# Output products and value products of two groups interleaved by tiling on TensorE

## The chip, the cores and the metric

The kernel runs on one core of a Trainium2 chip. The metric is the time of one execution on the device in microseconds (us), as the median of several runs. Five engines work side by side, each through its own queue in order: TensorE (PE, with its weight loads as PEld), VectorE (DVE), ScalarE (ACT), GpSimd (POOL) and SyncE (SP). PE writes into PSUM, from where ACT and DVE read; POOL and SP issue the transfers here.

## The reference

`x` is 8 x 4224 x 192, `weight_gen` 8 x 4224 x 8 x 7. A dynamic convolution (a softmax over 7 taps for each of 8 heads, applied to the last 7 rows of `x`) is followed by a gated product:

```python
w = np.exp(weight_gen - weight_gen.max(-1, keepdims=True)); w = w / (w.sum(-1, keepdims=True) + 1e-09)
x = np.einsum('bshk,bskhg->bshg', w, x_unf).reshape(B, S, D)   # x_unf: the last 7 rows
gate_pre = sum(conv_w[k] * xp[:, k:k + S, :] for k in range(5))  # xp: x with 4 zero rows ahead
gate = 1.0 / (1.0 + np.exp(-gate_pre))
val = x @ w_val
return gate * val @ w_out
```

## The kernel before

The sequence is cut into 36 **groups** of 118 rows, all 8 batches together. A group `m` goes through these steps:

- `load_x` (POOL, L410; three buffers `xt`) and `load_t` (SP, L424; two buffers `tb`) bring the rows of `x` and a banded matrix of softmax weights. The softmax itself runs ahead in ten parts on DVE and ACT; `spread` (ACT, L320) lays its result out in `zt`, a store (L327; SP for the first three parts, POOL after) puts it into the DRAM tensor `zd`, and `load_t` reads it from there.
- `bank` (PE, L437): the dynamic convolution as four sets of 32 small matmuls in a tiling of four column tiles, each set into a PSUM tile `pa` of which there are three. `evac` (ACT, L448 to L455) copies them to `A`, `B` and `S`; `move` (POOL, L464 and L466) transfers slices of `S` into `A` and `B`.
- `tap0` (ACT, L478), four `tap` (DVE, L483) and `sigm` (ACT, L488) make the gate, in `aA` for channels 0 to 127 and in `aB` for the other 64 (two batch halves above each other).
- `val` (PE): the product with `w_val` into the PSUM tiles `v2` and `v01` of which there is one each. L497 uses two column tiles of 64, L499 and L501 the whole array, L504 two row tiles of 64.
- `gv` (DVE, L511 and L513): gate times value, in place in `aA` and `aB`.
- `omm(k)`, `k` = 0 and 1 (PE): the product with `w_out`, two batches of each half at a time, into the PSUM tile `po`, of which there is one. Its part with `aA` (L524, four matmuls) uses the whole array, its part with `aB` (L531, four matmuls) two row tiles of 64. `oev(k)` (ACT, L546) copies `po` to `ot`, and `store` (SP, L555) writes the result.

Matrix products in float32 take two passes: the profile shows two instructions for each matmul.

The order on every engine is fixed by a planner, the class `Order`: steps are added with an engine, a duration, a key and the steps they depend on, and `run` plays them through with its own figures. On the engine that is free first it takes, among the steps that could begin within `SLACK` of the earliest, the one with the smallest key. `SWITCH` is what it adds when PE changes its tiling (`mode`), `RATE` and `LAND` are its figures for transfers. The order that comes out is what the engines execute; the waits are real semaphores. `val` depends on the `gv` of the group before, since `v2` and `v01` have one buffer; `omm(0)` depends on `gv` of its own group and on the last `oev` of the group before; `omm(1)` on `oev(0)`.

At the start POOL and DVE share the conversion of the two weight matrices (L210 to L221), which arrive as 64-bit numbers.

Of the kernel before, what the change touches and what calls it, by code (L numbers as in the profile page):

```python
# [16 lines left out]
class Order:  # L17
# [4 lines left out]
    SWITCH = 0.1  # L22
    SEM = 0.08
    RATE = 260e3
    LAND = {"SP": 2.8, "ACT": 2.8, "POOL": 3.8}
# [16 lines left out]
    def run(self):  # L42
# [6 lines left out]
        free, mode, dma = {}, {}, 0.0  # L49
# [6 lines left out]
        while done < len(self.ops):  # L56
            best = None
            for eng, c in open_.items():
                if not c:
                    continue  # L60
                t = free.get(eng, 0.0)
                first = min(max(t, o.ready) for _, o in c)
                n, o = min(((n, o) for n, o in c if max(t, o.ready) <= first + self.SLACK), key=lambda x: (x[1].key, x[0]))
                s = max(t, o.ready)
                if best is None or s < best[0]:
                    best = (s, n, o)
# [9 lines left out]
            if o.bytes:  # L76
                dma = max(dma, e + 0.8) + o.bytes / self.RATE
                o.end = dma + self.LAND[o.eng]
# [11 lines left out]
def tile_dynconv_gated_moe(  # L90
# [9 lines left out]
    nc = tc.nc  # L100
# [279 lines left out]
    class Group:  # L380
# [109 lines left out]
        def val(self):  # L490
            n = HB * self.n
            v2 = self.v2 = ps_v.tile([P, 512], FP32, name="v2")
            v01 = self.v01 = ps_v.tile([P, 2, 512], FP32, name="v01")
            A, Bt = self.part(0, HALO), self.part(1, HALO)
            A = [A[:, HB * u:HB * u + HB] for u in range(2)]
            for u in range(2):
                nc.tensor.matmul(out=v2[HD * u:HD * u + HD, 0:n], lhsT=wvm, rhs=A[u], start=True, stop=False,  # L497
                                 tile_position=(0, HD * u))
            nc.tensor.matmul(out=v2[:, 0:n], lhsT=wvd, rhs=Bt, start=False, stop=True)  # L499
            for u in range(2):  # L500
                nc.tensor.matmul(out=v01[:, u, 0:n], lhsT=wva, rhs=A[u], start=True, stop=False)  # L501
            for u in range(2):
                hs = slice(HD * u, HD * u + HD)
                nc.tensor.matmul(out=v01[:, u, 0:n], lhsT=wvb[hs], rhs=Bt[hs], start=False, stop=True,  # L504
# [10 lines left out]
        def omm(self, k):  # L515

            n = self.n
            po = self.po = ps_o.tile([P, 2, 512], FP32, name="po")

            def a_part(first):  # L520
                for u in range(2):
                    for t in range(2):
                        c = n * (HB * u + 2 * k + t)
                        nc.tensor.matmul(out=po[0:n, u, D * t:D * t + D], lhsT=self.aA[:, c:c + n], rhs=woa,  # L524
                                         start=first and t == 0, stop=not first, skip_group_check=True)

            def b_part(first):
                for t in range(2):
                    for u in range(2):
                        hs, c = slice(HD * u, HD * u + HD), n * (2 * k + t)  # L530
                        nc.tensor.matmul(out=po[0:n, u, D * t:D * t + D], lhsT=self.aB[hs, c:c + n], rhs=wob[hs],  # L531
                                         start=first and t == 0, stop=not first, skip_group_check=True,
                                         tile_position=(HD * u, 0))

            if k == 0:
                b_part(True)
                a_part(False)
            else:
                a_part(True)
                b_part(False)  # L540
# [84 lines left out]

    for i in range(3):
        soft_part(i)
    late_clear.behind.append(soft[1]["exp"])
    for m, gp in enumerate(gr):
# [58 lines left out]
        val = add("PE", 5 * mm(HB * n), m + 1.5, gp.val, [*full[0], *full[1], *placed, *dep(m - 1, "gv")], mode=("64c", "64r"))  # L688
# [39 lines left out]
```

## Time and profile before

| | us |
|---|---|
| median of 3 runs (lowest, highest) | 588.81 (587.95, 588.96) |
| profiled execution, its own time | 587.95 |
| its span | 586.2 |
| PE busy | 484.9 (83%) |
| DVE busy | 438.5 (75%) |
| ACT busy | 345.0 (59%) |
| POOL busy | 330.2 (56%) |
| L437 PE MATMUL `pa` x4608 | 140.5 |
| L524 PE MATMUL `po` x576 | 117.2 |
| L531 PE MATMUL `po` x576 | 68.6 |
| L497, L499, L501, L504 PE MATMUL `v` | 38.0, 39.3, 63.6, 38.1 |
| L546 ACT COPY `ot` x72, mean of one | 57.8, 0.803 |

Busy time counts what an engine executes, not what it waits; the ends of matmuls are modelled, so a row of a block can end 0.07 us after the next block has begun. A timeline row has start, length, engine, line, operation and count, and in brackets how long the engine stood idle ahead of it and what ended that.

### The profile page before, as it was taken

How to read it: one execution, taken by the hardware profiler on the slowest of the kernel's cores; microseconds unless marked ns; L12 is line 12 of the kernel's file. 1: busy time of each engine (PE TensorE's matmuls, PEld its weight loads, DVE VectorE, ACT ScalarE, POOL GpSimd, SP SyncE). 2: the span in 40 equal slices, each digit the busy share in tenths (PEclk: the TensorE clock that was granted, in tenths of full speed). 3: DMA queues.
4: the chain of work that ended last, by engine and by line, in shares of the span. 5: the costliest groups of instructions: out<-in, count | busy, mean ns of one | idle time of the engine just before them, and what ended most of it. 6: DMA issues, size and time to landing. Idle time of an engine off the chain costs nothing.

```text
span 586.2 us, 15839 instructions
## 1 busy us (share of the span) xinstructions
PE 484.9 (83%) x6278; PEld 327.0 (56%) x6278; DVE 438.5 (75%) x488; ACT 345.0 (59%) x533; POOL 330.2 (56%) x613
## 2 busy tenths in 40 slices
PE   2033868599848988999979997998999999999994
PEld 1033535386525764566746673765766675767653
DVE  6776396679857299898887889878975679667780
ACT  4435554478535667458666766586585656546641
POOL 9535956256470666657457455677576687522410
PEclk7557879799987999999979998999999999999999
DMA  5989689738799998879997989799789868775222
GB/s 156 213 239 242 144 223 257 200 99 236 216 236 228 283 266 243 207 207 246 290 259 187 267 217 275 212 261 252 194 217 259 248 158 200 205 183 164 66 60 89
DMA packets 105869, 123.17 MB, mean 210 GB/s; under 512 B 17938, under 2 KB 95615, under 8 KB 103107
## 3 DMA queue, kind: packets, MB, share of 16 engines
q1 hardware_dynamic: 79779, 65.40, 42.5%
q0 software_dynamic: 26016, 56.75, 36.1%
q8 instruction: 50, 0.82, 0.6%
q14 instruction: 24, 0.20, 0.1%
HBM read 64.55 MB, written 51.43 MB: 198 GB/s over the span
## 4 chain that ended last, share of the span: by engine, by line
PE 40%; DMA 30%; POOL 13%; issue 8%; ACT 4%; DVE 2%; SPq 1%; POOLq 0%; ACTq 0%; DVEq 0%
DMA zd<-zt 13%; PE po L524 10%; PE pa L437 10%; POOL xt L410 7%; DMA A<-S 6%; PE po L531 5%; DMA xt<-in_x_dram 5%; PE v L501 5%; DMA tb<-zd 3%; PE v L499 3%; PE v L504 3%; PE v L497 3%; POOL A L464 2%; DMA raw_c<-cd 1%; POOL B L466 1%
## 5 line engine op out<-in xcount | busy, mean ns | idle before, releaser
L483 DVE SCALAR_TENSOR_TENSOR aA<-A,wf,aA 128x944 f32<-128x944 f32 (+1 forms) x144 | 171.6, 1192 | 26.6 <-ACT aA L478 22.8
L437 PE MATMUL pa<-tb,xt 128*32 128x122 f32 (+1 forms) x4608 | 140.5, 276 | 48.8 <-DMA tb<-zd 43.1
L410 POOL DMA_DIRECT2D xt<-in_x_dram x272 | 143.8, 549 | 44.0 <-DMA A<-S 8.7
L437 PEld LDWEIGHTS pa<-tb,xt 128*32 128x32 f32 x4608 | 127.7, 110 | 64.0 <-issue 56.1
L483 DVE SCALAR_TENSOR_TENSOR aB<-B,wf,aB 128x472 f32<-128x472 f32 (+1 forms) x144 | 101.2, 703 | 46.2 <-ACT aB L478 39.0
L466 POOL DMA_DIRECT2D B<-S x144 | 74.7, 525 | 95.8 <-ACT B L451 83.5
L524 PE MATMUL po<-wf,aA 128*118 128x192 f32 (+1 forms) x576 | 117.2, 349 | 11.8 <-DVE aA L511 9.4
L524 PEld LDWEIGHTS po<-wf,aA 128*118 128x118 f32 (+1 forms) x576 | 94.6, 188 | 43.2 <-issue 20.1
L464 POOL DMA_DIRECT2D A<-S x144 | 74.2, 521 | 69.2 <-DMA zd<-zt 36.9
L546 ACT COPY ot<-po 118x768 f32<-118x768 f32 (+1 forms) x72 | 57.8, 803 | 82.3 <-PE po L531 49.4
L531 PE MATMUL po<-wf,aB 64*118 64x192 f32 (+1 forms) x576 | 68.6, 358 | 26.6 <-ACT ot L546 16.8
L531 PEld LDWEIGHTS po<-wf,aB 64*118 64x118 f32 (+1 forms) x576 | 45.8, 183 | 42.6 <-ACT ot L546 18.9
L501 PE MATMUL v<-A,wva 128*128 128x472 f32 (+1 forms) x144 | 63.6, 562 | 0.0
L455 ACT COPY S<-pa 64x488 f32<-64x488 f32 (+1 forms) x72 | 40.5, 562 | 31.1 <-PE pa L437 30.6
L488 ACT ACTIVATE aA<-aA 128x944 f32<-128x944 f32 (+1 forms) x36 | 35.5, 986 | 32.5 <-DVE aA L483 32.5
L511 DVE TENSOR_TENSOR aA<-v,aA 128x944 f32<-128x944 f32 (+1 forms) x36 | 40.7, 1130 | 13.7 <-PE v L504 8.1
L320 ACT COPY zt<-wt 128x192 f32<-128x192 f32 (+3 forms) x100 | 39.1, 461 | 17.5 <-DVE wt L308 11.4
L478 ACT ACTIVATE aA<-A,wf 128x944 f32<-128x944 f32 (+1 forms) x36 | 38.9, 1081 | 14.2 <-DMA A<-S 14.2
L501 PEld LDWEIGHTS v<-A,wva 128*128 128x128 f32 x144 | 27.7, 192 | 31.0 <-issue 30.4
L448 ACT COPY A<-pa 128x488 f32<-128x488 f32 (+1 forms) x72 | 40.5, 565 | 6.5 <-PE pa L437 5.3
L497 PE MATMUL v<-A,wvm 128*64 128x472 f32 (+1 forms) x144 | 38.0, 605 | 7.1 <-DMA A<-S 5.2
L499 PE MATMUL v<-B,wvd 128*128 128x472 f32 (+1 forms) x72 | 39.3, 627 | 0.0
(60 smaller groups left out, 367.5 us busy)
## 6 DMA issues: line engine op xcount, KB each, us to landing
xt<-in_x_dram POOLq DMA_DIRECT2D x272, 96.0 KB, 4.2
tb<-zd SPq DMA_DIRECT2D x285, 88.0 KB
out_dram<-ot SPq DMA_DIRECT2D x35, 672.0 KB
zd<-zt POOLq DMA_DIRECT2D x14, 1104.0 KB, 8.1
wt<-in_weight_gen_dram SPq DMA_DIRECT2D x6, 1120.0 KB
zd<-zt POOLq DMA_DIRECT2D x6, 920.0 KB, 7.5
A<-S POOLq DMA_DIRECT2D x140, 30.5 KB, 4.4
B<-S POOLq DMA_DIRECT2D x140, 15.2 KB, 4.8
```

Of the source, the lines that this page charges most:

```text
L410: nc.gpsimd.dma_start(out=self.xb[:, j, 0:D], in_=src)
L437: nc.tensor.matmul(out=pa[Q * c:Q * c + Q, w * j:w * j + w], lhsT=self.xb[:, u * HB + j, C * h:C * h + Q], rhs=self.t[:, u * HB + j, PAD / ...
L464: nc.gpsimd.dma_start(out=self.A[q:q + n], in_=self.S[p:p + n])
L466: nc.gpsimd.dma_start(out=self.B[HD * u + q:HD * u + q + n], in_=self.S[p:p + n, w * u:w * u + w])
L483: nc.vector.scalar_tensor_tensor(out=a, in0=self.part(g, j), scalar=cw[:, g, j:j + 1], in1=a, op0=ALU.mult, op1=ALU.add)
L497: nc.tensor.matmul(out=v2[HD * u:HD * u + HD, 0:n], lhsT=wvm, rhs=A[u], start=True, stop=False, tile_position=(0, HD * u))
L499: nc.tensor.matmul(out=v2[:, 0:n], lhsT=wvd, rhs=Bt, start=False, stop=True)
L501: nc.tensor.matmul(out=v01[:, u, 0:n], lhsT=wva, rhs=A[u], start=True, stop=False)
L511: nc.vector.tensor_tensor(out=a, in0=self.v01[:, :, 0:n], in1=a, op=ALU.mult)
L524: nc.tensor.matmul(out=po[0:n, u, D * t:D * t + D], lhsT=self.aA[:, c:c + n], rhs=woa, start=first and t == 0, stop=not first, skip_group_ ...
L531: nc.tensor.matmul(out=po[0:n, u, D * t:D * t + D], lhsT=self.aB[hs, c:c + n], rhs=wob[hs], start=first and t == 0, stop=not first, skip_g ...
L546: nc.scalar.copy(out=self.ot[0:n, :, 2 * k:2 * k + 2, :].rearrange("p u t d -> p u (t d)"), in_=self.po[0:n, :, 0:2 * D])
```

## The change

`val` is split into `val_c` (column tiles), `val_a` (whole array) and `val_b` (row tiles), and `omm` into `out_a` (whole array) and `out_b` (row tiles). A function `output(m, last)` adds the output products of a group; the two calls for group `m - 1` stand inside the value product of group `m`: after `val_a` comes `out_a(0)`, `out_b(0)`, then `val_b`, then `out_b(1)`, `out_a(1)`. `gv` of `aB` depends on `val_a` alone, that of `aA` on `val_b`. The planner counts a change of tiling already when it chooses, with 0.19 us in place of 0.1; it keeps a transfer figure for each queue, where it had one for all, and its rate and landing times are lower.

```diff
-    SWITCH = 0.1
+    SWITCH = 0.19
...
-    RATE = 260e3
-    LAND = {"SP": 2.8, "ACT": 2.8, "POOL": 3.8}
+    RATE = 200e3
+    LAND = {"SP": 2.4, "ACT": 2.4, "POOL": 3.2}
...
-                first = min(max(t, o.ready) for _, o in c)
-                n, o = min(((n, o) for n, o in c if max(t, o.ready) <= first + self.SLACK), key=lambda x: (x[1].key, x[0]))
-                s = max(t, o.ready)
+                now = mode.get(eng)
+                at = [(max(t, o.ready), (o.mode is not None and o.mode[0] != now) * self.SWITCH, n, o) for n, o in c]
+                first = min(s + w for s, w, _, _ in at)
+                s, _, n, o = min((a for a in at if a[0] + a[1] <= first + self.SLACK), key=lambda x: (x[3].key, x[2]))
...
-                dma = max(dma, e + 0.8) + o.bytes / self.RATE
-                o.end = dma + self.LAND[o.eng]
+                dma[o.eng] = max(dma.get(o.eng, 0.0), e + 0.8) + o.bytes / self.RATE
+                o.end = dma[o.eng] + self.LAND[o.eng]
...
+    def output(m, last):
...
+        d, gp = T[m], gr[m]
+        n, k = gp.n, len(d.setdefault("oev", []))
+        free = dep(m - 1, "oev")[-1:] if k == 0 else d["oev"][-1:]
+        a, f = m + 2.52 + 0.03 * k, (gp.out_a, gp.out_b)
+        o = [last] if last else []
+        for i, c in enumerate((k, 1 - k)):
+            o.append(add("PE", (4, 2)[c] * mm(D), a + 0.01 * i, lambda c=c, i=i: f[c](k, i == 0),
+                         [d["gv"][1 - c], conv["o"], *(free if i == 0 else [])], mode=(("128",), ("64r",))[c], behind=o[-1:]))
+        lent = dep(m - 3, "store") if m != 2 else [conv["o"], conv["v"]]
+        d["oev"].append(add("ACT", act(4 * D, True), m + 1.2, lambda: gp.oev(k), [o[-1], *(lent if k == 0 else [])]))
...
-        val = add("PE", 5 * mm(HB * n), m + 1.5, gp.val, [*full[0], *full[1], *placed, *dep(m - 1, "gv")], mode=("64c", "64r"))
-        gv = [add("DVE", dve(size[g]), m + 2.0, lambda gp=gp, g=g: gp.gv(g), [val, sg[g]]) for g in (1, 0)]
...
-        for k in range(2):
-            o.append(add("PE", 6 * mm(D), m + 2.1 + 0.3 * k, lambda gp=gp, k=k: gp.omm(k),
-                         [*gv, conv["o"], *(evs[-1:] if k else dep(m - 1, "oev")[-1:])], mode=(("64r", "128"), ("128", "64r"))[k]))
...
+        gv1 = dep(m - 1, "gv")
+        vc = add("PE", mm(HB * n), m + 1.5, gp.val_c, [*full[0], *full[1], *placed, *gv1], mode=("64c",))
+        va = add("PE", 3 * mm(HB * n), m + 1.51, gp.val_a, [*gv1], mode=("128",), behind=[vc])
+        mid = output(m - 1, va) if m else va
+        vb = add("PE", mm(HB * n), m + 1.54, gp.val_b, [], mode=("64r",), behind=[mid])
+        if m:
+            output(m - 1, vb)
+        d["gv"] = [add("DVE", dve(size[g]), m + 2.0, lambda gp=gp, g=g: gp.gv(g), [(vb, va)[g], sg[g]]) for g in (1, 0)]
+        d["useA"], d["useB"] = [va, tp[0][-1]], [vb, tp[1][-1]]
+    output(NM - 1, output(NM - 1, None))
```

Since the planner's figures and its choice change, the order changes on all engines, not at the moved products alone. Two places follow. In the rows of an order `x4` counts equal instructions in a row, and each matmul stands once.

PE, around the value product 22 (counted from 0), before: L437 is a bank, L531 and L524 are the `aB` and `aA` parts of an output product, L497 to L504 the value product.

```order
L437 MATMUL pa<-tb_76,xt_82 32x122 x64
L531 MATMUL po<-wf,aB 118x192 x4
L524 MATMUL po<-wf,aA 118x192 x4
L497 MATMUL v_3912<-A,wvm 64x472 x2
L499 MATMUL v_3912<-B,wvd 128x472
L501 MATMUL v_3913<-A,wva 128x472 x2
L504 MATMUL v_3913<-B,wvb 128x472 x2
L524 MATMUL po<-wf,aA 118x192 x4
L531 MATMUL po<-wf,aB 118x192 x4
```

The same engine with the change, around the same value product (the second L498): L438 is the bank, L498, L503 and L506, L512 are `val_c`, `val_a`, `val_b`, L531 is `out_a` and L542 `out_b`.

```order
L438 MATMUL pa<-tb_75,xt_81 32x122 x64
L438 MATMUL pa<-tb_76,xt_82 32x122 x64
L498 MATMUL v_3801<-A,wvm 64x472 x2
L503 MATMUL v_3801<-B,wvd 128x472
L506 MATMUL v_3810<-A,wva 128x472 x2
L531 MATMUL po<-wf,aA 118x192 x4
L542 MATMUL po<-wf,aB 118x192 x4
L512 MATMUL v_3810<-B,wvb 128x472 x2
L542 MATMUL po<-wf,aB 118x192 x4
L531 MATMUL po<-wf,aA 118x192 x4
L498 MATMUL v_3876<-A,wvm 64x472 x2
```

Blocks of one tiling now stand beside each other (L503, L506 and L531; L542, L512 and L542), two banks follow each other, and the two output products of a group are `val_b` apart where a whole value product or a bank lay between them.

POOL at the start of the program, before: `xt` are loads of `x`, `B<-S` and `A<-S` are moves (the first eight are the first group's), L214 to L220 convert `w_out`.

```order
L466 DMA B<-S 8x488 x2
L410 DMA xt_82<-in_x_dram 128x1x192 x8
L466 DMA B<-S 8x488 x2
L464 DMA A<-S 8x976 x4
L410 DMA xt_80<-in_x_dram 128x1x192 x8
L214 TENSOR_SCALAR wf<-wf 128x2x192
L466 DMA B<-S 8x488 x4
L218 TENSOR_SCALAR aA<-aA 128x2x192
L219 TENSOR_SCALAR aA<-aA 128x2x192
L220 TENSOR_TENSOR wf<-wf,aA 128x2x192
```

The same place with the change; the conversion has the lines L215 to L221, the loads L411, the moves L467 and L465.

```order
L411 DMA xt_81<-in_x_dram 128x1x192 x8
L215 TENSOR_SCALAR wf<-wf 128x2x192
L411 DMA xt_82<-in_x_dram 128x1x192 x8
L219 TENSOR_SCALAR aA<-aA 128x2x192
L220 TENSOR_SCALAR aA<-aA 128x2x192
L221 TENSOR_TENSOR wf<-wf,aA 128x2x192
L467 DMA B<-S 8x488 x4
L411 DMA xt_80<-in_x_dram 128x1x192 x2
L465 DMA A<-S 8x976 x4
```

The conversion of `w_out` has moved ahead of the first group's moves, and these stand behind one more set of loads.

More of the change, by code (lines that the diff above doesn't have):

```diff
@@ L48, in run @@
                 d.users.append((o, False))
-        free, mode, dma = {}, {}, 0.0
+        free, mode, dma = {}, {}, {}
         open_ = {}
@@ L488, in sigm, with rows_of, val_c, val_a @@
             nc.scalar.activation(out=a, in_=a, func=AF.Sigmoid)
-        def val(self):
+        def rows_of(self, u):
+            return self.part(0, HALO)[:, HB * u:HB * u + HB]
+        def val_c(self):
+            self.v2 = ps_v.tile([P, 512], FP32, name="v2")
+            for u in range(2):
+                nc.tensor.matmul(out=self.v2[HD * u:HD * u + HD, 0:HB * self.n], lhsT=wvm, rhs=self.rows_of(u),
+                                 start=True, stop=False, tile_position=(0, HD * u))
+        def val_a(self):
             n = HB * self.n
[L492 to L495, printed above, removed]
+            nc.tensor.matmul(out=self.v2[:, 0:n], lhsT=wvd, rhs=self.part(1, HALO), start=False, stop=True)
+            self.v01 = ps_v.tile([P, 2, 512], FP32, name="v01")
             for u in range(2):
[L497 to L501, printed above, removed]
+                nc.tensor.matmul(out=self.v01[:, u, 0:n], lhsT=wva, rhs=self.rows_of(u), start=True, stop=False)
+        def val_b(self):
+            Bt = self.part(1, HALO)
             for u in range(2):
                 hs = slice(HD * u, HD * u + HD)
-                nc.tensor.matmul(out=v01[:, u, 0:n], lhsT=wvb[hs], rhs=Bt[hs], start=False, stop=True,
+                nc.tensor.matmul(out=self.v01[:, u, 0:HB * self.n], lhsT=wvb[hs], rhs=Bt[hs], start=False, stop=True,
                                  tile_position=(HD * u, 0))
@@ L624, in soft_part @@
             softmax(r0, R, at - 5.5, at - 2.2, at - 7.0, at - 1.7)
+    def output(m, last):
[9 more added lines that the diff above has]
+        d["oev"].append(add("ACT", act(4 * D, True), m + 1.2, lambda: gp.oev(k), [o[-1], *(lent if k == 0 else [])]))
+        d["out"] = o[-2:]
+        if k:
+            d["store"] = [add("SP", 0.55, m + 2.0, lambda i=i: gp.store(i), d["oev"], delay=4.0,
+                              bytes=n * D * 4 * (B if i == 0 else 1)) for i in range(2)]
+        return o[-1]
     for i in range(3):
```

45 lines of the change are left out of this document (17 added, 28 removed).

## The prediction

> **What bounds the kernel now.** I read the chain that ended last first, then cut the span at the value products (`val`, first line L497) and read the busy time of each stretch.
>
> ```profile
> PE 40%; DMA 30%; POOL 13%; issue 8%; ACT 4%; DVE 2%; SPq 1%; POOLq 0%; ACTq 0%; DVEq 0%
> 201.90:402.48 200.58, 184.59 (x2422) 123.05 (x2420) 171.52 (x186) 135.07 (x203) 126.81 (x244) 0.97 0.89 242
> 402.48:567.67 165.19, 163.40 (x2135) 109.72 (x2134) 124.11 (x138) 97.33 (x151) 89.63 (x172) 1.00 0.70 183
> ...
> 201.90 1.01 PE L497 MATMUL v<-A,wvm 128*64 128x472 f32 x4
> ...
> 402.48 1.01 PE L497 MATMUL v<-A,wvm 128*64 128x472 f32 x4
> ...
> 567.67 0.86 PE L497 MATMUL v<-A,wvm 128*64 128x376 f32 x4
> ```
>
> The columns of the two stretches are length, then busy time of PE, weight load, DVE, ACT and POOL, the granted clock, the DMA share and GB/s. The three rows below them (start, us) are where value products 8, 22 and 35 begin, counted from 0: 14 groups in the first stretch, 13 in the second. The **last stretch** is PE's alone: 163.40 of 165.19 us busy, 12.71 us a group. The **middle stretch** takes 14.33 us a group: PE stands idle for 16.0 us, and the DMA engines are busy 0.89 of the time. Before 201.90 there is the **start**, where supply decides. The chain inside the last stretch shows one full group (start, us, what):
>
> ```profile
> 422.41 3.68 PE pa L437 x121
> 426.09 0.84 PE po L531 x8
> 426.94 1.49 PE po L524 x8
> 428.43 0.94 PE v L497 x4
> 429.37 0.99 PE v L499 x2
> 430.36 1.59 PE v L501 x4
> 431.95 0.99 PE v L504 x4
> 432.94 1.49 PE po L524 x8
> 434.43 0.84 PE po L531 x8
> 435.27 3.68 PE pa L437 x121
> ```
>
> The pieces follow each other without a hole, so the group costs 435.27 - 422.41 = 12.86 us and every nanosecond between blocks counts.
>
> **The price of a change of tiling.** L501 is the one block that follows a block of its own tiling (L499, both on the whole array): 1.59 / 4 = 0.3975 us for 472 columns. L499 has two such steps, 0.795, and takes 0.99: 0.19 too much. L504 has four matmuls, two by two beside each other, again 0.795 against 0.99. For 192 columns the step is 0.3975 x 192/472 = 0.162; L524 with eight is 1.29 against 1.49, L531 with four pairs 0.65 against 0.84. So each entry into another tiling costs **0.19 us** in four different blocks.
>
> The Trainium skill, "TensorE: Matmul & The Clock Gate", section "Step-by-step: what each phase is for", gives about 128 cycles for the last column to leave the array. At the full 2.4 GHz of that page that is an estimate of 0.053 us for a drain, and 100 changes saved would then be 5.3 us, less than the hand-over below takes: this change would lose. The rows above say 0.19, and they decide.
>
> **What the change removes.** In the planned order PE changes its tiling 284 times before and 184 times after (counted over all rows of blocks): 62, 111 and 111 in start, middle and last stretch against 44, 70 and 70. Per group three entries go: that of the first L524, of L504, and of the last L531. 100 x 0.19 = **19.0 us**, 7.8 of it in each of the two later stretches (41 x 0.19).
>
> **What it adds: a hand-over with little cover.** `po` is one buffer. The second output product may start only when ACT has copied the first one out (L546, `oev`). Before, a bank (3.68) or a whole value product (4.5) stood between; now mostly only `val_b`. At the very end of the kernel the trace has the bare hand-over:
>
> ```profile
> 572.88 0.91 PE L531 MATMUL po<-wf,aB 64*118 64x192 f32 x8
> 573.84 0.80 ACT L546 COPY ot<-po 118x768 f32<-118x768 f32 x1 [2.72 <-PE po L531]
> 574.69 0.89 PE L531 MATMUL po<-wf,aB 64*94 64x192 f32 x8 [0.90 <-ACT ot L546]
> ```
>
> From the start of the block to the earliest next output is 574.69 - 572.88 = 1.81 us with an ACT that stands ready. In the new order this block takes 0.65 (no change of tiling behind it) and `val_b` 0.80, so PE comes back after 1.45 and waits **0.36 us**. In the order this stands directly so at 26 places (4 in the start, 11 in each later stretch); at the other ten a bank or part of one stands between. 26 x 0.36 = 9.4 us. Bounds: 0, if the modelled ends are late by as much, and per place 1.04 when ACT is at another instruction, as here:
>
> ```profile
> 155.37 0.91 PE L531 MATMUL po<-wf,aB 64*118 64x192 f32 x8
> 156.15 0.98 ACT L488 ACTIVATE aA<-aA 128x944 f32<-128x944 f32 x1
> 157.03 0.78 ACT L546 COPY ot<-po 118x768 f32<-118x768 f32 x1
> 157.86 0.91 PE L531 MATMUL po<-wf,aB 64*118 64x192 f32 x8 [0.59 <-ACT ot L546]
> ```
>
> This one took 157.86 - 155.37 = 2.49, which is 0.68 more. I take 0.36, since ACT mostly stands waiting for the block:
>
> ```profile
> ACT ot L546 <- PE po L531: 49.4, 27, 3.7
> ACT ot L546 <- PE po L524: 30.9, 28, 4.0
> ```
>
> That is 55 of 72 copies. Behind a waiting output product on PE stand the rest of the outputs, the next bank and the next `val_c`; nothing can pass them.
>
> **Sums by stretch.** Last: 7.8 - 11 x 0.36 = **-3.8**. Middle: the same -3.8 if PE were all; but its 16.0 us of idle time come from others:
>
> ```profile
> PE po L524 <- DVE aA L511: 6.8, 4, 2.9
> PE po L531 <- DVE aB L513: 4.1, 2, 3.4
> ```
>
> 10.9 of it is waiting for the products on DVE. A PE that is sooner waits longer at these places, so between 0 and -3.8 I take half, **-1.9**. In the new order pairs of banks stand ahead of two value products, which gives taps and moves a group more of lead, so the bound on this side is -16 more; the DMA share of 0.89 speaks against taking any of it, since 14.33 x 0.89 = 12.75 us of transfers a group leave no room below 12.75.
>
> **The start.** The planner's new figures for changes and transfers reorder all queues. On POOL the conversion of `w_out` (L214 to L220) moves ahead of the first moves, and all of them behind the loads of `xt`:
>
> ```profile
> 62.84 0.51 POOL L214 TENSOR_SCALAR wf<-wf 128x384 f32<-128x384 uint32 x1
> 68.64 1.03 POOL L220 TENSOR_TENSOR wf<-wf,aA 128x384 f32<-128x384 f32 x1
> 69.71 0.56 DVE L221 SCALAR_TENSOR_TENSOR wf<-ot,wf 128x384 uint32<-128x384 uint32 x1 [9.63 <-POOL wf L220]
> 76.39 1.08 POOL L327 DMA_DIRECT2D zd<-zt  x2 [0.42 <-DMA xt<-in_x_dram]
> 120.68 3.75 PE L437 MATMUL pa<-tb,xt 128*32 128x122 f32 x128
> ```
>
> DVE stands 9.63 us behind that conversion with the first group's taps behind it, so up to 9.6 can be won. Late next is the fourth group's bank (120.68), whose weights leave POOL from 76.39 on; the new order puts the second of these stores behind another group's eight moves, which can lose as much. Between -9.6 and +9.6 I take a third of the gain, **-3**, because the removed wait is certain and the new one has the 44 us to 120.68 as cover. The drain is as before: two bare hand-overs after the last `gv`, and the stores. The new split of `val` adds no instruction, and `gv` has in both orders the outputs and, mostly, a bank to finish before the next value product.
>
> Sum: -3.8 - 1.9 - 3 = **-8.7 us** on the profiled execution's 587.95 us (span 586.2): 579.3. The median of the runs shown is 0.86 higher, 588.81, so I predict 580.1 for a median.
>
> **Rivals.**
> *Supply holds start and middle.* Then only the last stretch gains: 588.81 - 3.8 = 585.0. For it: the DMA share of 0.89 and
>
> ```profile
> q1 hardware_dynamic: 79779, 65.40, 42.5%
> q0 software_dynamic: 26016, 56.75, 36.1%
> ```
>
> two queues that share 16 engines, where the new planner gives each 200 GB/s of its own, 400 together, against 242 in the middle stretch. Against it: PE is 92% busy there.
>
> *A load planned too early parks PE.* The same figures make an order in which a bank stands ahead of a value product that is ready, while its load is not there. One such stall is in the trace, there by ACT:
>
> ```profile
> 168.75 0.91 PE L531 MATMUL po<-wf,aB 64*118 64x192 f32 x8
> 177.45 1.64 PE L531 MATMUL po<-wf,aB 64*118 64x192 f32 x8 [7.79 <-ACT ot L546]
> 179.52 2.77 PE L524 MATMUL po<-wf,aA 128*118 128x192 f32 x8 [0.43 <-DVE aA L511]
> ```
>
> 7.79 of waiting and, the blocks running slower after it, 1.64 - 0.91 and 2.77 - 1.49 (the chain's L524), 2.0 more: 9.8. Two of them make 588.81 - 8.7 + 19.6 = 599.7. Deciding point: one such stall cancels the forecast. The Trainium skill, "Trainium Kernel Development and Optimization", section "Key Constraints", says that transfers issued from SP, ACT and POOL interleave on the same 16 engines, and that several queues save issue time alone; by that rule the planner's 400 GB/s cannot be had and this rival and the one before gain. The 242 GB/s agree.
>
> *The hand-over is late.* If ACT is behind by 0.68 at each of the 26 places, they cost 26 x 1.04 = 27.0, more than the 19.0 saved: +8.0, 596.8. It decides from 19.0 / 26 = 0.73 us per place, that is 0.37 us of lateness on average. For it: up to 17 of 72 copies found ACT at other work, and there was much cover until now. Against it: the planner sets the copy where it expects the block's end.
>
> *The order does not save the entries*, because blocks of one tiling still drain when `po` and `v` change: no gain, and 9.4 lost, 598.2. Against it: L501 behind L499.
>
> **How the numbers follow.** Forecast 0.50, supply 0.20, late hand-over 0.20, parked PE 0.08, no entries saved 0.02. A difference under 0.2% (1.2 us) can't be told from none. Faster: 0.50 and 0.14 of the supply case; within 0.2%: 0.06 of the supply case and 0.02 of the late hand-over where costs cancel; slower: the rest, 0.28. Range: below, the whole gain of both stretches and the start with its full 9.6 is 588.81 - 7.6 - 9.6 = 571.6, and a little of the middle's idle time on top, 569; above, the late hand-over, 596. The forecast's own range is 571 to 587.
>
> **What would show it.** Right: a full group in the last stretch of about 12.86 - 3 x 0.19 + 0.36 = 12.65 us at a direct place; `val_b` at 0.80 where L504 had 0.99; waits of PE for `ot` near 0.36 at some 26 places; DVE's 9.63 gone. Wrong: waits for `ot` above 0.73 on average, a wait of PE for `tb` above 5 us after 100 us, a middle stretch still at 14.3 us a group with the DMA share above 0.9, or a fourth bank later than 121 us.

## The result and the profile after

The change is slower: 603.46 us median (600.75 to 606.89, 4 runs) against 588.38 (587.70 to 588.96, 4 runs) of the kernel before beside it. The ratio is 1.026, interval 1.0205 to 1.0315. The prediction was 580.1, with a range from 569 to 596. The profiled execution took 606.89 us, its span is 605.1 where before had 586.2, and its mean granted clock 0.917 where before had 0.932.

The chain that ended last, from the page of the changed kernel:

```profile
DMA 41%; PE 25%; POOL 13%; DVE 7%; issue 7%; ACT 6%; SPq 0%; POOLq 0%; ACTq 0%; DVEq 0%
```

PE held 40% of the chain before; now transfers hold 41%. The busy time by stretch, the changed kernel cut at the same value products as in the prediction (columns as there):

```profile
0.00:186.34 186.34, 120.32 (x1630) 80.51 (x1631) 138.65 (x161) 105.42 (x168) 113.62 (x197) 0.84 0.82 214
186.34:403.86 217.52, 185.09 (x2436) 132.31 (x2437) 161.43 (x177) 130.18 (x199) 124.80 (x239) 0.94 0.84 221
403.86:584.34 180.48, 162.82 (x2135) 113.66 (x2134) 129.59 (x147) 103.72 (x161) 92.56 (x178) 0.97 0.69 184
```

| stretch | before | after | difference | predicted |
|---|---|---|---|---|
| start (to value product 8) | 201.9 | 186.3 | -15.6 | -3 |
| middle (8 to 22) | 200.6 | 217.5 | +16.9 | -1.9 |
| last (22 to 35) | 165.2 | 180.5 | +15.3 | -3.8 |
| end | 18.5 | 20.8 | +2.2 | 0 |

The stretches do not hold quite the same work. By the count of matmuls on `po`, the change has two output products fewer in the start (112 instructions of L542 for 128 of L531), one more in the middle and one more in the end; in the last stretch the count is the same. An output product takes PE 1.49 + 0.84 = 2.33 us in a steady group, so I estimate that 4.7 us of the gain of the start, 2.3 of the loss of the middle and all of the end are blocks that changed sides of a cut. The rest is real. In the last stretch PE is busy 162.82 of 180.48 us: the 1.8 us of idle time before have become 17.7. The DMA engines have not become fuller there (share 0.70 before, 0.69 after), nor has PE got more work. The waits of PE, largest first (us in total, times, longest), changed kernel:

```profile
PE pa L438 <- DMA tb<-zd: 43.9, 4, 31.5
PE po L542 <- ACT ot L550: 19.8, 9, 6.8
PE v L498 <- DMA A<-S: 15.8, 4, 7.9
PE pa L438 <- ACT S L456: 15.2, 9, 6.3
PE v L498 <- DMA xt<-in_x_dram: 8.4, 2, 6.2
PE v L498 <- issue: 5.4, 1, 5.4
```

Most of the loss is in a few places and not spread over all groups. PE has seven stalls of over 4 us behind 100 us, all its rows of that kind in the timeline of the changed kernel (start, length, what, in brackets the idle time ahead and what ended it):

```profile
134.71 1.85 PE L438 MATMUL pa<-tb,xt 128*32 128x122 f32 x32 [6.29 <-ACT S L456]
155.82 1.84 PE L498 MATMUL v<-A,wvm 128*64 128x472 f32 x4 [5.36 <-issue]
219.94 4.96 PE L438 MATMUL pa<-tb,xt 128*32 128x122 f32 x96 [7.17 <-DMA tb<-zd]
307.14 1.64 PE L542 MATMUL po<-wf,aB 64*118 64x192 f32 x8 [6.84 <-ACT ot L550]
382.77 1.64 PE L542 MATMUL po<-wf,aB 64*118 64x192 f32 x8 [4.33 <-ACT ot L550]
451.27 1.84 PE L498 MATMUL v<-A,wvm 128*64 128x472 f32 x4 [6.25 <-DMA xt<-in_x_dram]
511.47 4.22 PE L438 MATMUL pa<-tb,xt 128*32 128x122 f32 x96 [4.90 <-DMA tb<-zd]
```

Before had two of that size there, 6.42 and 7.79 us, both in the start; its middle and last stretch have none. Each costs more than its idle time, since the blocks behind it run slower: 1.84 for L498, which takes 1.01 in a steady group, 4.96 for 96 instructions of a bank that take 2.87. The profile shows the clock that was granted in these rows: 0.50 from 307.14 to 308.78 and from 451.27 to 454.78, and 1.00 again from 457.27 on. Three of the seven end with the landing of a load (`tb`, `xt`, `tb`), two with ACT's copy `ot`. In the middle stretch the wait for `ot` is PE's largest: 15.1 us, where before has 0.2. What ACT did ahead of 307.14 is in the next two fences, first ACT's timeline, then PE's:

```profile
301.18 0.69 ACT L479 ACTIVATE aB<-B,wf 128x472 f32<-128x472 f32 x1 [6.21 <-DMA B<-S]
304.44 1.08 ACT L479 ACTIVATE aA<-A,wf 128x944 f32<-128x944 f32 x1 [2.57 <-DMA A<-S]
305.44 0.97 ACT L489 ACTIVATE aA<-aA 128x944 f32<-128x944 f32 x1
306.31 0.78 ACT L550 COPY ot<-po 118x768 f32<-118x768 f32 x1
```

```profile
298.60 0.91 PE L542 MATMUL po<-wf,aB 64*118 64x192 f32 x8
299.34 0.96 PE L512 MATMUL v<-B,wvb 64*128 64x472 f32 x4
307.14 1.64 PE L542 MATMUL po<-wf,aB 64*118 64x192 f32 x8 [6.84 <-ACT ot L550]
```

The first output product is done at 299.5. Its copy, 0.78 us of work, begins at 306.31, because ACT's order has two first taps ahead of it, and these waited 6.21 and 2.57 us for their moves to land.

### The profile page after: what moved, and what is told of

The parts are those of the page before. It is cut to its first block, busy times and chain, and to the rows that moved or that the text cites. A ratio compares the mean times of both kernels' runs of the same rounds, so it can differ in the third digit from the quotient of the medians.

```text
span 605.1 us, 15838 instructions
## 1 busy us (share of the span) xinstructions
PE 481.1 (80%) x6278; PEld 335.4 (55%) x6278; DVE 433.7 (72%) x488; ACT 344.7 (57%) x533; POOL 331.0 (55%) x613
## 4 chain that ended last, share of the span: by engine, by line
DMA 41%; PE 25%; POOL 13%; DVE 7%; issue 7%; ACT 6%; SPq 0%; POOLq 0%; ACTq 0%; DVEq 0%
DMA xt<-in_x_dram 12%; DMA A<-S 12%; DMA zd<-zt 8%; PE pa L438 7%; DMA B<-S 6%; PE po L531 6%; POOL xt L411 4%; PE po L542 4%; PE v L506 3%; POOL A L465 3%; DVE aA L484 2%; POOL B L467 2%; ACT ot L550 2%; PE v L503 2%; PE v L498 2%
## 5 line engine op out<-in xcount | busy, mean ns | idle before, releaser
L438 PE MATMUL pa<-tb,xt 128*32 128x122 f32 (+1 forms) x4608 | 144.7, 282 | 64.4 <-DMA tb<-zd 43.9
L438 PEld LDWEIGHTS pa<-tb,xt 128*32 128x32 f32 x4608 | 132.9, 113 | 80.9 <-issue 58.6
L411 POOL DMA_DIRECT2D xt<-in_x_dram x272 | 143.7, 549 | 49.1 <-DMA A<-S 17.0
L467 POOL DMA_DIRECT2D B<-S x144 | 74.6, 525 | 102.5 <-ACT B L452 90.3
L465 POOL DMA_DIRECT2D A<-S x144 | 74.1, 520 | 71.3 <-DMA zd<-zt 26.9
L531 PE MATMUL po<-wf,aA 128*118 128x192 f32 (+1 forms) x576 | 111.5, 337 | 0.9 <-ACT ot L550 0.9
L531 PEld LDWEIGHTS po<-wf,aA 128*118 128x118 f32 (+1 forms) x576 | 95.3, 184 | 24.7 <-issue 23.1
L542 PE MATMUL po<-wf,aB 64*118 64x192 f32 (+1 forms) x576 | 67.1, 352 | 21.7 <-ACT ot L550 19.8
L542 PEld LDWEIGHTS po<-wf,aB 64*118 64x118 f32 (+1 forms) x576 | 44.8, 180 | 51.8 <-ACT ot L550 41.7
L506 PE MATMUL v<-A,wva 128*128 128x472 f32 (+1 forms) x144 | 65.7, 578 | 0.3 <-DVE aA L519 0.3
L498 PE MATMUL v<-A,wvm 128*64 128x472 f32 (+1 forms) x144 | 40.5, 641 | 29.8 <-DMA A<-S 15.8
L521 DVE TENSOR_TENSOR aB<-v,aB 128x472 f32<-128x472 f32 (+1 forms) x36 | 23.1, 642 | 38.7 <-ACT aB L489 23.9
L479 ACT ACTIVATE aB<-B,wf 128x472 f32<-128x472 f32 (+1 forms) x36 | 24.8, 689 | 44.9 <-DMA B<-S 38.5
L449 ACT COPY A<-pa 128x488 f32<-128x488 f32 (+1 forms) x72 | 40.7, 565 | 12.6 <-PE pa L438 11.7
L456 ACT COPY S<-pa 64x488 f32<-64x488 f32 (+1 forms) x72 | 40.5, 563 | 12.6 <-PE pa L438 12.1
L506 PEld LDWEIGHTS v<-A,wva 128*128 128x128 f32 x144 | 28.9, 201 | 33.9 <-issue 30.4
```

The costliest lines, as they stand in the source:

```text
L411: nc.gpsimd.dma_start(out=self.xb[:, j, 0:D], in_=src)
L438: nc.tensor.matmul(out=pa[Q * c:Q * c + Q, w * j:w * j + w], lhsT=self.xb[:, u * HB + j, C * h:C * h + Q], rhs=self.t[:, u * HB + j, PAD / ...
L449: nc.scalar.copy(out=self.A[:, w * kind:w * kind + w], in_=pa[:, 0:w])
L465: nc.gpsimd.dma_start(out=self.A[q:q + n], in_=self.S[p:p + n])
L467: nc.gpsimd.dma_start(out=self.B[HD * u + q:HD * u + q + n], in_=self.S[p:p + n, w * u:w * u + w])
L479: nc.scalar.activation(out=a.rearrange("p (b n) -> p b n", n=n), in_=self.part(g, 0), func=AF.Copy, scale=cw[:, g, 0:1])
```

## The experiments

Four theories were held against each other. **T**, the tie: the outputs of a group may run only behind `val_a` of the next group, so they can no longer fill PE's time while that value product waits for its moves. **F**, the figures: the new rate, landing times and clocks of the transfers make an order that expects data too early; its part **F1** (in the last run **Q**) blames the separate clock of each queue alone. **N**, no cause in the content: the order before is a lucky draw of the planner, and any reordering of all engines loses. "Untied" below means outputs that wait for their own gates only. The expectations have three more names: B is an earlier name of T; **H** blames the hand-over of `po` without cover, **P** pairs of banks that the new choice lines up. All medians are in us; ratios are to runs of the kernel before on the same chip, with 95% intervals.

**One part of the change at a time.** `e1_old_figures`: the change, with the planner's transfer figures as before.

```diff
-    RATE = 200e3
-    LAND = {"SP": 2.4, "ACT": 2.4, "POOL": 3.2}
+    RATE = 260e3
+    LAND = {"SP": 2.8, "ACT": 2.8, "POOL": 3.8}
...
-        free, mode, dma = {}, {}, {}
+        free, mode, dma = {}, {}, 0.0
...
-                dma[o.eng] = max(dma.get(o.eng, 0.0), e + 0.8) + o.bytes / self.RATE
-                o.end = dma[o.eng] + self.LAND[o.eng]
+                dma = max(dma, e + 0.8) + o.bytes / self.RATE
+                o.end = dma + self.LAND[o.eng]
```

> The changed kernel with the old transfer figures of the planner (one shared rate of 260 GB/s, landing 2.8 and 3.8); products moved and change of tiling counted as in the change. Theory F (the new transfer figures plan tap0 on ACT before the moves have landed, and ACT holds back oev and evac): ACT's waits for DMA A<-S and B<-S fall from 69 us to below 45, time 575 to 588. Theory H (the bare hand-over alone makes every lateness of ACT one of PE): it has 32 direct places, more than the change's 26, so 598 to 606. Theory P (pairs of banks): the order has fewer pairs, 588 to 596.

`e2_figures_only`: the kernel before with this diff the other way round and nothing else. `e3_choice_only`: the kernel before with `SWITCH = 0.19` and the choice that counts a change of tiling. `e4_products_only`: the split and moved products, the planner as before.

> The kernel before with the new transfer figures alone. Theory F: ACT's waits for moves rise from 31 us to 45 to 70, time 593 to 605. Theory H: 586 to 591, since oev keeps its cover. Theory P: 586 to 591.

> The kernel before with the planner's new choice alone (change of tiling counted when choosing, at 0.19). Its order has 261 changes of tiling in place of 284. Theory P (the choice lines up pairs of banks, which empties both tb buffers and delays moves): 593 to 602. Theories F and H: 584 to 589.

> The moved products alone, planner as before. Its order has 239 changes of tiling and 5 direct places, elsewhere part of a bank stands between. Theory F: 582 to 588. Theory H: 584 to 589, since a part of a bank is in nearly all hand-overs. Theory P: 582 to 588. If it is above 592, the moved products themselves cost, for another reason than the bare hand-over.

| run | median | ratio |
|---|---|---|
| e1 | 602.11 | 1.0196 (1.0141 to 1.0252) |
| e2 | 598.11 | 1.0138 (1.0074 to 1.0201) |
| e3 | 583.28 | 0.9876 (0.9836 to 0.9915) |
| e4 | 600.45 | 1.0173 (1.0110 to 1.0236) |

The choice gains; the products alone lose, and the figures alone lose too. With the old figures the products still lose 2%, so F is not the whole; with the old products the figures lose 1.4%, so T is not either. P would have e3 at 593 or more, and H would have e4 at 589 or less; both are refuted as the whole cause.

**The tie.** `e5_products_free` is e4, `e6_all_free_old_figures` is e1 and `e9_change_free` is the change, each with the outputs untied and `val_b` behind `val_a`:

```diff
-        o = [last] if last else []
+        o = []
...
-        vb = add("PE", mm(HB * n), m + 1.54, gp.val_b, [], mode=("64r",), behind=[mid])
+        vb = add("PE", mm(HB * n), m + 1.54, gp.val_b, [], mode=("64r",), behind=[va])
```

> As e4 (moved products, planner as before), but the outputs of group m-1 no longer have to stand behind val_a and val_b of group m: the planner may put them where their own data is ready. Theory B (an output tied behind a value product can't fill PE's time while that product waits for its moves): PE's waits for moves and for gv ahead of val_c (31 and 14 us in e4) fall below 25 together, time 585 to 593 against 600 in e4. Rival N (any new order of this chaotic plan loses 1 to 2% whatever it ties): 596 to 604. Rival H (bare hand-over): 4 direct places as against 5 in e4, so no change, 598 to 602.

> As e1 (moved products, new choice, old figures), outputs free as in e5. 197 changes of tiling, 20 direct places against 177 and 32 in e1. Theory B: 580 to 590 against 602 in e1. Rival N: 597 to 605. Rival H: 12 direct places fewer at 0.27 give 599.

> The change as it is, with one part undone: the outputs are no longer tied behind val_a and val_b. 188 changes of tiling, 24 direct places. Theory B: 588 to 596 (the tie costs what e1 to e6 and e4 to e5 showed, 13 to 16 us; the new figures keep their 8 us of e2). Theory F alone: 599 to 606, the wait for moves on ACT above 60 us as in the change. Rival N (chance of the order): anywhere from 585 to 604 with no tie to PE's waits for moves.

e5 took 587.37 (0.9959, 0.9916 to 1.0002), e6 585.79 (0.9932, 0.9896 to 0.9969), e9 613.28 (1.0392, 1.0341 to 1.0442). Under the old figures untying wins back 13 us of e4 and 16 of e1. Waits of PE at the value product, e4 and then e5:

```profile
PE v L497 <- DMA A<-S: 31.3, 8, 6.7
PE v L497 <- DVE aB L520: 13.9, 3, 6.0
```

```profile
PE v L497 <- DVE aB L520: 13.3, 3, 8.2
PE v L497 <- DMA A<-S: 5.6, 2, 3.1
```

That looked like proof of T, and e9 took it back: in the change itself untying costs another 10 us. Whatever loses there is not cured by free outputs.

**Later landing.** If orders that expect data too early lose, orders that expect it later might gain. `e7_choice_late_moves` is e3 and `e8_free_late_moves` is e6 with longer landing times:

```diff
-    LAND = {"SP": 2.8, "ACT": 2.8, "POOL": 3.8}
+    LAND = {"SP": 3.4, "ACT": 3.4, "POOL": 4.8}
```

> The kernel before with the new choice (583 in e3) and landing times that are later than the old figures (3.4 for SP and ACT, 4.8 for POOL; shared rate 260 GB/s), near the measured 4.1 to 4.9 of the moves. Theory F read on (later figures put tap0 behind what can run meanwhile): ACT's waits for moves below 25 us, 574 to 583. If figures do no more than reshuffle: 578 to 592, without fewer waits for moves.

> e6 with the later landing times of e7. Theories B and F together: 572 to 583. If one of them is wrong, no better than the better of e6 and e7.

e7 took 598.91 (1.0137, 1.0067 to 1.0207), 16 us more than e3; e8 593.05 (1.0050, 1.0020 to 1.0080), 7 more than e6. Later landing is no cure.

**Separate clocks, and reorderings without a meaning.** `e10_queue_only` is the kernel before with a transfer clock for each queue (the last three pairs of lines of e1's diff, the other way round). `e11_neutral_slack` is the kernel before with `SLACK` 0.10 for 0.08, `e12_neutral_sem` with `SEM`, the planner's figure for a semaphore, 0.10 for 0.08. Neither says anything about a transfer or a product; both shuffle every engine's order.

> The kernel before with a transfer clock for each queue, but the old rate and landing times. Theory F1 (what plans moves too early is that two queues no longer share a rate): 594 to 602, ACT's waits for moves above 50 us as in e2 (97). Theory F2 (it is the shorter landing times): 585 to 591, waits near 31.

> The kernel before with SLACK 0.10 in place of 0.08, a change without any meaning for the hardware, which reshuffles the order (275 changes of tiling). Theory N: it differs from 589 by 1% or more, so that single orders say little. Theories B and F: within 0.8%, 584 to 594.

> The kernel before with SEM 0.10 in place of 0.08, as meaningless (287 changes of tiling). Theory N: differs from 589 by 1% or more. Theories B and F: within 0.8%, 584 to 594.

e10 took 609.82 (1.0333, 1.0279 to 1.0387), e11 602.36 (1.0217, 1.0158 to 1.0276), e12 604.47 (1.0231, 1.0186 to 1.0275). So a reordering without a meaning can cost 2.2 to 2.3%, as much as most of the losses above; of the runs so far e9 (3.9%) and e10 (3.3%) lie above that, and two draws do not say how far such losses can go. Nor does every reordering lose, as N has it: e3, e5 and e6 have new orders and are no slower than before. The same two shuffles of the change, `e15_change_slack` and `e16_change_sem`:

> The change with SLACK 0.10, as e11 for before. Theory N: somewhere from 585 to 615, the mean of this, e16 and the change near that of e11, e12 and before or below. Theory T: 600 to 612 for each, above e11 and e12 by what the tie costs.

> The change with SEM 0.10, as e12 for before. As e15: theory N 585 to 615, theory T 600 to 612.

603.87 (1.0234, 1.0179 to 1.0289) and 604.32 (1.0252, 1.0202 to 1.0303): three draws of the changed program lie within 1 us of each other. Beside e11 and e12 it is the order before that stands out, not that of the change.

**The order held fixed.** Therefore the next runs keep the planner's order of before on every engine and change only what PE executes in it. `e13_swap_fixed_order` lets the second output product begin with its `aB` part as the first one does, which takes away 23 of the 284 changes of tiling:

```diff
-            if k == 0:
-                b_part(True)
-                a_part(False)
-            else:
-                a_part(True)
-                b_part(False)
+            b_part(True)
+            a_part(False)
```

> The kernel before, every engine's order kept, but the second output product runs its aB part first (beside the aB part of the value product), as in the change. 23 changes of tiling fewer, no hand-over without cover. If an entry costs 0.19 us and PE bounds: 23 x 0.19 = 4.4 us in all, 584 to 587. Theory T (the tie of outputs behind the value product) and theory N (another order loses) say nothing against it. If the entries are not worth 0.19: 588 to 591.

586.54 (0.9933, 0.9900 to 0.9966): 3.4 us less by the medians, 3.9 by the ratio, against 23 x 0.19 = 4.4. The price of a change of tiling holds as a gain in time.

`e14_products_fixed_order` and `e17_products_fixed_one_copy` have the change's arrangement on PE, tie included, in the order of before: where a value product stood between the two output products of a group, the first of them goes behind `val_a` (27 places, 202 changes of tiling for 284).

```diff
+            elif what == "val":
+                gp.val_c()
+                gp.val_a()
+                h = held.pop(m - 1, [])
+                if h:
+                    g = h[0].tag[1]
+                    g.out_a(0, True)
+                    g.out_b(0, False)
+                    g.oev(0)
+                gp.val_b()
```

> The kernel before with the change's arrangement on PE (value product in three parts, first output product between val_a and val_b, second behind val_b, tied as in the change), the order of DVE, POOL and SP kept row for row, ACT's too except for the copies that move with their product. 202 changes of tiling against 284, 29 direct places. Theory N (the change lost because the planner drew another order): 82 x 0.19 - 29 x 0.27 = 7.8 us gained, 579 to 585. Theory T (outputs tied behind a value product that waits for its moves or for gv): PE's waits at val_c for moves and gv rise by 20 us or more as in e4, 595 to 606.

e14 took 605.90 (1.0268, 1.0222 to 1.0313), what T asked for. But it had a fault. The groups of e14 (mean length behind the busy time) have 99 copies of `po` where the output needs 72:

```profile
L624 ACT COPY ot<-po 118x768 f32<-118x768 f32 (+1 forms) x99 | 76.9, 802 | 138.7 <-PE po L589 108.9 <-PE po L578 29.7
L589 PE MATMUL po<-wf,aB 64*118 64x192 f32 (+1 forms) x576 | 65.7, 346 | 25.8 <-ACT ot L624 25.6
```

At each of the 27 places the copy stood at its new place and again at the old one, and PE waited for both. 27 copies of some 0.75 us are 20 us. e14 says nothing about T. e17 is e14 with one copy:

```diff
+                    if what == "oev" and at[("omm", gp, 0)] < at[nxt[0]]:
+                        continue
```

> The kernel before with every engine's order kept, but PE's output products arranged as in the change: where a value product stood between a group's two output products, the first of them moves behind the value product's whole-array block, the value product's last block behind it, the second output product behind that (27 places, 202 changes of tiling where before has 284). This is the run e14 once more without its fault: e14 copied the first output product out of po a second time at these 27 places (99 copies of po where every other kernel has 72), about 0.75 us each on the hand-over, which alone are some 20 us. Theory T (tied outputs cost long stalls, whatever the order): the stalls of PE for the moves and for DVE, 34 us in e14 against 20 us in before, stay: 595 to 606. Theory N (the arrangement is sound, and the change lost by the planner's new order on all engines, as any reordering of before does): entries -82 x 0.19 = -15.6, hand-over 27 x 0.27 = +7.3, some of it in stretches where PE waits anyway: 578 to 586. Between 587 and 594 both have a part.

590.63 (1.0020, 0.9995 to 1.0045): no difference from before, in the gap between the two, where both were to have a part. Its stretches and its waits of PE:

```profile
0.00:200.62 200.62, 124.61 (x1662) 85.17 (x1663) 138.79 (x161) 109.06 (x177) 114.24 (x199) 0.83 0.81 213
200.62:401.33 200.71, 180.04 (x2405) 123.24 (x2405) 168.35 (x181) 129.83 (x199) 123.44 (x237) 0.96 0.89 239
401.33:565.91 164.58, 160.89 (x2134) 110.55 (x2135) 124.33 (x137) 95.97 (x152) 92.21 (x178) 1.00 0.71 184
```

```profile
PE v L530 <- DVE aB L570: 24.5, 5, 9.4
PE v L530 <- DMA A<-S: 11.4, 3, 6.3
PE pa L470 <- ACT S L488: 6.8, 7, 2.2
PE v L538 <- DVE aA L568: 6.5, 5, 2.2
```

In the middle stretch PE is busy 4.5 us less than before (184.59 to 180.04) and the stretch is as long (200.58 and 200.71), with the DMA share at 0.89 as before. Some 2.3 us of this is an output product that now stands behind the cut (416 matmul instructions on `po` for 434); the rest is saved, and all of it has become waiting. In the last stretch, with the same work, PE is busy 2.5 us less and 0.6 is left. Before, PE met DVE's lateness at the outputs (9.4 and 9.9 us in the whole run, none at the value product) and ACT's at `ot` (19.2). In e17 it meets DVE's at the value product (24.5 and 6.5), where nothing can pass, and the waits for `ot` are down to 2.9. The lateness is met at another place, and PE's saving goes into it. How much of that is the tie and how much supply that could not come sooner anyway, e17 does not separate; together they take the gain of the arrangement and no more.

**The change with one clock.** `e18_change_one_clock` is the change with its own rate and landing times, but one clock for all queues (the last three pairs of lines of e1's diff alone).

> The change whole, with one thing undone: its planner again has one transfer clock for all queues (at the change's own 200 GB/s and landing times) where the change gives each queue a clock of its own. Theory Q (the loss of the change in the last stretch, 180.5 us from value product 22 to 35 against 165.2 in before, is loads that the separate clocks plan too late: PE's waits for xt and tb there, 6.2 and 4.9 us): the last stretch comes back to 160 to 168 us and no wait of PE for a load above 3 us is left in it; the middle stretch, where the tied outputs stand too, between 200 and 213; in all 580 to 595. Rival (the tie of the outputs, or any new order as such, as in the two neutral reorderings that cost 2.2%): the last stretch stays at 172 or more, in all 600 or more.

607.56 (1.0307, 1.0277 to 1.0338). Q's forecast for the whole (580 to 595) was missed, and the rival's (600 or more) came; Q's forecast for the last stretch was met. The stretches of e18:

```profile
0.00:211.76 211.76, 121.19 (x1631) 83.89 (x1631) 154.33 (x175) 114.52 (x188) 116.68 (x201) 0.80 0.82 217
211.76:424.80 213.04, 186.79 (x2437) 130.04 (x2437) 164.21 (x178) 127.74 (x199) 123.85 (x238) 0.94 0.83 223
424.80:585.18 160.38, 159.01 (x2138) 111.49 (x2134) 119.48 (x132) 92.62 (x140) 90.86 (x176) 1.00 0.71 173
```

The last stretch takes 160.38 us, 20 less than in the change and 4.8 less than before, and PE is idle for 1.4 us of it. The start takes 25.4 us more than in the change, so with the separate clocks undone the loss has moved and not gone. Work moved with it: DVE has 154.33 us to do in this start against 138.65 in that of the change, and 119.48 against 129.59 in the last stretch. PE's longest wait after the first bank in the start is 10.71 us, for ACT's copy `S`; why this order pays there is not shown. ACT's waits at the first tap for the moves, of the change and then of e18:

```profile
ACT aB L479 <- DMA B<-S: 38.5, 15, 6.2
ACT aA L479 <- DMA A<-S: 30.9, 20, 3.3
```

```profile
ACT aA L479 <- DMA A<-S: 3.9, 3, 2.2
ACT aB L479 <- DMA B<-S: 3.3, 3, 1.6
```

This wait divides the runs. ACT's listed waits for the moves at a first tap come to 7 to 36 us in every run with one clock (before 30.8), and to 72 to 97 us in every run with one for each queue (the change 72.5, e2 96.6, e10 71.6). The length of the last stretch, cut in the same way, divides them as well:

| clock | last stretch (us), value products 22 to 35 |
|---|---|
| one for all | before 165.2, e1 166.5, e3 164.8, e4 167.0, e5 163.8, e6 159.8, e7 159.9, e8 158.3, e11 167.7, e12 162.6, e13 164.5, e17 164.6, e18 160.4 |
| one for each queue | change 180.5, e2 172.5, e9 177.9, e10 171.9, e15 176.8, e16 175.3 |

(e14, with its extra copies, has 171.1.) It is not that a stretch which begins later finds its data there: e10 begins it at 421.5 us and takes 171.9, before begins it at 402.5 and takes 165.2. With the products as before the border is narrower than it looks, since e3 has a bank and an output product fewer in this stretch: by PE's idle time there, e3 has 6.8 us, e10 6.9 and e2 8.9. With the products moved it is wide: 1.4 to 6.4 us in the runs with one clock, 13.4 to 17.7 in the change, e9, e15 and e16.

What the separate clocks do ahead of the stall at 451.27 can be read on POOL, in the change:

```profile
433.10 1.08 POOL L328 DMA_DIRECT2D zd<-zt  x2
442.11 0.53 POOL L411 DMA_DIRECT2D xt<-in_x_dram  x1 [4.75 <-DMA zd<-zt]
449.27 0.52 POOL L411 DMA_DIRECT2D xt<-in_x_dram  x1 [6.64 <-DMA zd<-zt]
```

Two stores of softmax parts stand ahead of a set of loads of `xt`; POOL issues the last two loads only when these stores have landed, and the eight loads take 15.5 us to land at the median, where the page has 4.5 for the whole run. In the change six of the 25 such stores are issued in the last stretch, in e18 none; it is 5 or 6 in every run with separate clocks, and 0 to 3 in every other but e3, which has 5. No run moves these stores alone, so that they are the step between is read from the traces and not tested. The middle stretch has no such border:

| middle stretch (us), value products 8 to 22 | |
|---|---|
| order of before | before 200.6, e13 201.4, e17 200.7 |
| new order, products as before | e3 195.7, e7 211.1, e11 208.8, e12 218.4; separate clocks: e2 220.0, e10 219.4 |
| new order, products moved, untied | e5 204.2, e6 204.3, e8 206.2; separate clocks: e9 226.4 |
| new order, products moved, tied | e1 212.4, e4 214.8, e18 213.0; separate clocks: change 217.5, e15 219.2, e16 215.2 |

## Why the prediction was wrong

**The price of a change of tiling was nearly right.** e13 got 3.4 to 3.9 us for 23 of them, 0.15 to 0.17 each, where 0.19 each make 4.4. **The full group was right**: predicted 12.65 us, measured 12.66. Rows of e18's timeline on PE:

```profile
450.10 1.01 PE L498 MATMUL v<-A,wvm 128*64 128x472 f32 x4
451.05 1.06 PE L503 MATMUL v<-B,wvd 128*128 128x472 f32 x2
451.95 1.75 PE L506 MATMUL v<-A,wva 128*128 128x472 f32 x4
453.54 1.46 PE L531 MATMUL po<-wf,aA 128*118 128x192 f32 x8
454.93 0.91 PE L542 MATMUL po<-wf,aB 64*118 64x192 f32 x8
455.67 0.96 PE L512 MATMUL v<-B,wvb 64*128 64x472 f32 x4
456.74 0.91 PE L542 MATMUL po<-wf,aB 64*118 64x192 f32 x8
457.58 1.56 PE L531 MATMUL po<-wf,aA 128*118 128x192 f32 x8
459.07 3.76 PE L438 MATMUL pa<-tb,xt 128*32 128x122 f32 x128
462.76 1.01 PE L498 MATMUL v<-A,wvm 128*64 128x472 f32 x4
```

462.76 - 450.10 = 12.66, where before needs 12.86. **The hand-over was right with an ACT that stands ready**: 456.74 - 454.93 = 1.81 us from the start of the block to the next, the sum taken from the end of the kernel before. PE comes back after 0.74 + 0.80 and waits 0.27, where I had 0.36. That the group agrees to the hundredth is in part luck: with 0.27 for the wait the same sum gives 12.56, and three entries at 0.16 bring it back to 12.65.

**The term for the hand-overs was too small.** In the changed kernel the places are 26, as counted, and 20 of them cost 0.26 to 0.41 us (from the starts of L512 and L542, less 0.80). At the other six ACT was elsewhere, as at 307.14, and they cost 0.87 to 7.0. Together that is 24.7 us, 0.95 a place, where the term had 9.4 and 0.36 and would have turned the forecast at 0.73. So "ACT mostly stands waiting for the block" did not hold, and the cost of the rival "the hand-over is late" came nearly as priced (27.0). 17.5 of the 24.7 us are in the middle stretch. It does not explain the loss, though: e15, the change with another `SLACK`, has 24 such places and 9.8 us in all, near the term, 3.8 of it in the middle stretch, and is as slow as the change (603.87, the middle 219.2).

**What failed is the step "Sums by stretch".** It took the saving of a steady group times the number of groups and let everything else stand as before, and it gave the new figures an effect on the start alone. They reorder all engines up to the end of the program.

- *Last stretch*, predicted -3.8, measured +15.3. The separate clocks are the cause in this stretch, by experiment: undone in the change (e18) the stretch falls to 160.4, -4.8 against before, near the -3.8 of the sum; and every run with them has at least 171.9, every other at most 167.7, e14 aside. In the trace this is PE at a bank whose `tb` has not landed (4.90 us) and at a value product whose wait ends with the landing of an `xt` (6.25 us; the product does not read `xt`, and why it waits for this load the trace does not say), and ACT at taps whose moves have not landed. With the slower blocks behind them (1.84 + 1.94 + 2.65 for 1.01 + 1.06 + 1.75, and 4.22 for 2.87) the two stalls come to 15.1 of the 20.1 us between the change and e18. It is the rival "a load planned too early parks PE", with its mechanism, its 400 GB/s and its two stalls, put at 19.6. That its time is near too (599.7 against 603.46) is luck, since the start and the middle came out 12.6 us better and 18.8 worse than its sum had them. I gave it 0.08, with one such stall in the trace before. But that trace comes from an order made with one clock, so its count of such stalls says little of an order made with several. The sentence on the Trainium skill ("Trainium Kernel Development and Optimization", section "Key Constraints") stood on the right side: e10, with nothing but separate clocks, loses 3.3%, though shuffles without a meaning lose 2.2 and 2.3%.
- *Middle*, predicted -1.9, measured +16.9, of which some 2.3 is an output product that came over the cut. With the order of before the arrangement gives nothing here (e17, +0.1 with one output product fewer). That is the rival "supply holds start and middle"; the half of the saving that I took was still too much. The rest of the loss is the new order. Which property of it, stays **open**: separate clocks (e2, e10), the tie under the old figures (e4 and e1 against e5 and e6, 8 to 11 us) and a meaningless shuffle (e11, e12, 8 to 18 us) each lengthen the stretch by about half of what the change does, or more, and untying the change makes it worse (e9). Only the order of before and e3 stay at 201.4 us or less.
- *Start*, predicted -3, measured -15.6, of which some 4.7 is the shift of two output products across the cut. The rest comes from the figures: e2, with nothing else, has 180.5 there, with one output product fewer than before. It seems to take the separate clocks together with the new rate and landing: with the clocks alone the start is 202.0 (e10), in the change without them 211.8 (e18). DVE's wait of 9.63 for the conversion went as foretold, to 4.1 at the most.
- *Cover for the value product.* I wrote that `gv` has in both orders outputs and mostly a bank to finish ahead of the next value product. The change puts just these outputs behind it. In e17 that is 24.5 + 6.5 us of waits for DVE at the value product, where before has none listed. In the order of the change itself it is 0.5 us.

Of the marks named beforehand, the waits for `ot` (0.95 on average, the mark was 0.73) and the wait for `tb` above 5 us after 100 us (7.17 at 219.94) came out on the wrong side. The middle stretch did so in its length alone (217.5 / 14 = 15.5 us a group, the mark was 14.3): its DMA share was 0.84, where the mark asked for over 0.9 and before had 0.89, so the transfer engines were not fuller there. The bank that stood at 120.68 before is done earlier, from 105.49 on, on the right side.

The fastest kernel of the study is e3, the change's choice rule without its products and figures: 583.28 against 603.46 and 588.38. Since shuffles without meaning move this kernel by 2%, its 1.2% may be the rule or the draw; that was not separated.

## What to carry to other kernels

Where a planner makes the order, a new figure in it is a change of every engine up to the last group: predict it by the waits that the order can create, not by the stretch where its rows differ most, and measure it first with the order held fixed and against a shuffle that means nothing. A saving in a steady group is worth its count only where that engine has no other wait; ask of each piece that is moved which wait it filled at its old place. Count an experiment's instructions before its time is believed: the time of e14 agreed with the theory, and its doubled copy made it. Count them in each stretch too before stretches are compared.

## What the runs showed that was not expected

- A change of `SLACK` or `SEM` by 0.02 us, which is no change of the work, costs the kernel before 2.2 and 2.3% (e11, e12), more than the effect that was to be measured. The same two changes move the changed kernel by under 1 us (e15, e16).
- A stall is dearer than its idle time. Behind the seven waits of 4.33 to 7.17 us the first block ran at a granted clock of 0.50 to 0.62: L498 took 1.84 for 1.01, a bank behind 7.17 us of waiting 4.96 for 2.87, and behind 451.27 three blocks together lost 2.6 us.
- The wait between two output products is 0.27 us behind a cover of 0.80, but with one more copy of 0.75 us in the hand-over (e14) it is listed at 30 places with 25.6 us, 0.85 each.
